# Top-k attention and two feed-forward layers on one core: float64 weights converted through PSUM, attention outputs in the score banks

## The chip, the cores and the metric

The kernel runs on one core of one Trainium2 chip. The metric is the device time of one execution in microseconds (us). Five instruction queues run side by side, each in its own fixed order: TensorE (PE, with its weight loads shown apart as PEld), VectorE (DVE), ScalarE (ACT), GpSimd (POOL) and SyncE (SP), which issues the DMAs. An instruction waits for others through semaphores, and everything behind it in its queue waits with it.

## The reference

```python
def _attn_ref(q, k, v):                      # batch 4, heads 8, seq 576, head_dim 64
    scores = scale * np.matmul(q, k.transpose(0, 1, 3, 2))
    kth = np.partition(scores, -32, axis=-1)[..., -32:-31]
    scores = np.where(scores >= kth, scores, -1e9)
    attn = softmax(scores)
    return np.matmul(attn, v).astype(np.float32)
def _moe_ref(x, w_in, w_out):                # 2304 tokens, 512 -> 2048 -> 512
    h = x @ w_in
    return (np.maximum(0.01 * h, h) @ w_out).astype(np.float32)
def _moe2_ref(x, w1, w2, w3, w_out):         # 512 -> 768 -> 512
    h = np.maximum(np.maximum(x @ w1, x @ w2), x @ w3)
    return (h @ w_out).astype(np.float32)
```

The attention output, laid out as 2304 tokens by 512, goes through the two layers one after the other. The weights of both layers come as float64.

## The kernel before, in words

**Attention** is cut into 72 steps. A step takes two score tiles of 128 query rows by 576 keys (two heads of one block of 128 tokens, or four heads of a block of 64). PE computes the scores into the PSUM tile `s`, two banks of which columns 0 to 287 are used (L702); ACT copies them to `S` in SBUF (L707); DVE finds the 32nd largest value of every row by 8 MAX8 and 6 MATCH_REPLACE8 instructions of 576 columns (L722, L724, 14 in all), masks one exponential (L777) and makes a mask for the other (L781); POOL multiplies and splits (L784, L788); a transposing DMA makes `pt` (L791); PE multiplies by V into the PSUM tile `av`, one bank (L816 to L818); DVE makes the reciprocals `r` of the row sums from it (L823, L825), and ACT scales it into `xs` (L827).

**The feed-forward layers** run in 10 units of 128 to 256 tokens. Each has a phase H (PE: `h<-xu,wi`, then `acc<-f16t,wo`) and a phase M (PE: `h<-k,w`, a maximum over three products on DVE at L1000, then `acc<-f16t,w`). PE multiplies in two-part float16 (`three`, L859 to L861). Unit 0 begins phase H only when all chunks of `w_in` and `w_out` are ready, and phase M only when those of w1, w2, w3 and the second `w_out` are; phase H of unit 1 waits for the last of these too.

**The weights** come in 42 pieces: 16 of 1024 columns (kinds "i" and "o", `w_in` and `w_out`), 18 of 512 (kind "t") and 8 of 384 (kind "z"). `prep_w` loads a piece as 64-bit words (L478) and makes float32 bits of it by three integer instructions on DVE, each over the whole piece, which read every second 32-bit word of it: L484 (one tensor in, a shift and an and), L487 and L490 (two tensors in: the loaded words and the result so far). All operands lie in SBUF. ACT and PE then find a norm (L505, L511), DVE reduces it (L516, L326), POOL makes a scale of it (`pow2`, L333), and ACT and POOL write the two float16 parts (`split3`, L352 to L354).

**The order** of every queue is set by the planner `Plan`. Each `op` has an engine, an estimated duration, keys that it reads and writes and a priority; `run` simulates the queues and writes the instructions in the order of their simulated starts. Buffers are limited by `NB`. For a weight instruction the estimate is `dve(n)`, with its first argument the columns. The planner treats `s` and `av` as two buffers; which instruction waits for which in the built program is found afterwards, from the memory that they touch, by the framework under it.

PSUM has 8 banks of 512 float32 columns: `s` 2, `av` 1, `acc` 2, `h` 3. The tiles `h` serve the products, and the small sums of `total` and the norms as well.

Of the kernel before, what the change touches and what calls it, by code (L numbers as in the profile page):

```python
# [9 lines left out]
F32 = mybir.dt.float32  # L10
# [17 lines left out]
PS = 2048.0  # L28
# [191 lines left out]
def attention_moe_kernel(ctx, tc, qk, v, w_in, w_out, w123, w2o, outT):  # L220
# [11 lines left out]
          "s": 1, "av": 1, "acc": 2, "h": 3, "junk": 1, "xcap": 2, "pr": 8, "ph": 4, "ra": 3, "fi": 6, "ft": 9, "rw": 3, "fz": 3, "rc": 2, "hH": 3, "hM": 3, "kH": 2, "kM": 5, "fH": 2, "fM": 2}  # L232
# [45 lines left out]
    NCOL = 318  # L278
    colt = cp.tile([P, NCOL], F32, name="colt")
# [179 lines left out]
    SC = {}  # L459
    PRW0 = -13.5  # L460
    GATES = {1: [("d", 0, 0, 0, 1)], 2: [("d", 0, 1, 0, 1)]}

    def prep_w(kind, c, parts, hi, lo, colnorm, n2c, s, bi, pr, tags, guard=((), (), []), gate=()):
# [8 lines left out]
        for i, saps in enumerate(parts):  # L472
# [3 lines left out]
            for sap, n in saps:  # L476
# [5 lines left out]
                w = lambda raw=raw, n=n: raw().bitcast(I32)[:, :2 * n].rearrange("p (n t) -> p n t", t=2)  # L482
                t = lambda f=f, n=n, o=o: f()[:, o:o + n]
# [3 lines left out]
                op(DVE, dve(n), lambda w=w, t=t: V.scalar_tensor_tensor(  # L487
                    t(), w()[:, :, 0], 29, t(), op0=ALU.logical_shift_right, op1=ALU.bitwise_or),
                   r=[raw] + zr + zf, w=[(f, o)], pr=pr)
                op(DVE, dve(n), lambda w=w, t=t: V.scalar_tensor_tensor(  # L490
                    t(), w()[:, :, 1], -0x40000000, t(), op0=ALU.bitwise_and, op1=ALU.bitwise_or),
                   r=[raw] + zr + zf, w=[(f, o)], pr=pr)
# [187 lines left out]
    def attention(i):  # L680
# [119 lines left out]
        av = lambda: avb()[:, :260].rearrange("p (h e) -> p h e", e=65)  # L800
        for j in range(2):
            vt = VT[b, hps[j]]

            def avm(j=j, vt=vt):
                hs = [(j, slice(0, P), j)] if full else [(hh, slice(64 * hh, 64 * hh + 64), 2 * j + hh)
                                                        for hh in range(2)]
                for hh, qs, a in hs:
                    o = av()[:qs.stop - qs.start, a, :]
# [14 lines left out]
        op(DVE, 0.07, lambda: V.tensor_scalar(r()[:n, 0:nh], av()[:n, 0:nh, 64:65].rearrange("p h e -> p (h e)"),  # L823
                                             1e-9 * PS, None, op0=ALU.add), r=[avb], w=[(r, 0)], pr=pr)
        op(DVE, 0.08, lambda: V.reciprocal(r()[:n, 4:4 + nh], r()[:n, 0:nh]), r=[(r, 0)], w=[(r, 1)], pr=pr)  # L825
        for h in range(nh):
            op(ACT, act(64, True, 1), lambda h=h: A.activation(xs()[:n, h], av()[:n, h, 0:64], AF.Copy,  # L827
                                                              scale=r()[:n, 4 + h:5 + h]),
               r=[avb, (r, 1)], w=[(xs, h)], pr=pr)
# [343 lines left out]
```

## Time and profile before

| | |
|---|---|
| median of 3 runs | 1165.75 us (1165.68 to 1166.59) |
| the profiled execution | 1165.0 us, span of its trace 1163.2 us |
| busy in that span | PE 923.0, DVE 998.8, ACT 758.5, POOL 728.9 us |
| mean granted TensorE clock | 0.899 of full speed |

Busy times are sums over the span, so the table says nothing of when an engine was busy; the stretches in the rows below do. A line number is that of the kernel before; `w`, `k`, `raw` are names of SBUF tiles, `colt` a tile of single columns.

### The profile page before, as it was taken

How to read it: one execution, taken by the hardware profiler on the slowest of the kernel's cores; microseconds unless marked ns; L12 is line 12 of the kernel's file. 1: busy time of each engine (PE TensorE's matmuls, PEld its weight loads, DVE VectorE, ACT ScalarE, POOL GpSimd, SP SyncE). 2: the span in 40 equal slices, each digit the busy share in tenths (PEclk: the TensorE clock that was granted, in tenths of full speed). 3: DMA queues.
4: the chain of work that ended last, by engine and by line, in shares of the span. 5: the costliest groups of instructions: out<-in, count | busy, mean ns of one | idle time of the engine just before them, and what ended most of it. 6: DMA issues, size and time to landing. Idle time of an engine off the chain costs nothing.

```text
span 1163.2 us, 27290 instructions
## 1 busy us (share of the span) xinstructions
PE 923.0 (79%) x10294; PEld 807.4 (69%) x10294; DVE 998.8 (86%) x2106; ACT 758.5 (65%) x1625; POOL 728.9 (63%) x1054
## 2 busy tenths in 40 slices
PE   3252234675389899789899978998999999999998
PEld 2131223664289788678788867887988898898987
DVE  3999999999999999899996999989989999994001
ACT  7666566777567766547777865677787667564341
POOL 5577885797546766547777664567787557464231
PEclk9965555796589999899999999999999999999999
DMA  7756518554563543334466433554473332332000
GB/s 229 250 150 219 181 25 234 158 140 113 123 148 66 103 81 69 63 71 117 95 163 160 86 73 61 101 128 107 98 177 87 82 82 55 69 69 56 15 1 19
DMA packets 268548, 125.78 MB, mean 108 GB/s; under 512 B 237440, under 2 KB 255360, under 8 KB 266368
## 3 DMA queue, kind: packets, MB, share of 16 engines
q1 hardware_dynamic: 268416, 124.04, 43.4%
q8 instruction: 81, 1.33, 0.5%
q14 instruction: 51, 0.42, 0.1%
HBM read 62.65 MB, written 14.16 MB: 66 GB/s over the span
## 4 chain that ended last, share of the span: by engine, by line
PE 51%; DVE 20%; POOL 8%; ACT 7%; DMA 7%; issue 4%; SPq 1%; POOLq 0%; ACTq 0%; DVEq 0%
PE h L859 9%; PE h L860 9%; PE h L861 9%; DMA pt<-phl 6%; PE acc L860 5%; PE acc L861 5%; PE acc L859 5%; DVE m L722 5%; DVE w L724 4%; PE s L702 3%; DVE w L487 3%; DVE w L490 2%; POOL phl L788 2%; PE av L816 2%; DVE w L484 2%
## 5 line engine op out<-in xcount | busy, mean ns | idle before, releaser
L722 DVE MAX8 m<-w 128x8 f32<-128x576 f32 x432 | 310.2, 747 | 0.3
L916 POOL TENSOR_TENSOR f16t<-k,f16t 128x256 f16<-128x256 f32 (+2 forms) x220 | 143.4, 654 | 183.6 <-ACT f16t L910 174.9
L788 POOL TENSOR_TENSOR phl<-pp,phl 128x576 f16<-128x576 f32 x144 | 189.8, 1325 | 36.3 <-ACT phl L786 35.2
L724 DVE MATCH_REPLACE8 w<-m,w 128x576 f32<-128x576 f32 x288 | 212.1, 741 | 0.0
L859 PE MATMUL h<-k,w 128*128 128x256 f16 (+2 forms) x720 | 189.9, 268 | 22.1 <-ACT k L956 8.3
L860 PE MATMUL h<-k,w 128*128 128x256 f16 (+2 forms) x720 | 190.0, 268 | 5.2 <-POOL k L958 4.8
L861 PE MATMUL h<-k,w 128*128 128x256 f16 (+2 forms) x720 | 190.1, 268 | 0.0
L860 PE MATMUL acc<-f16t,wo 128*128 128x256 f16 (+2 forms) x640 | 167.3, 265 | 7.7 <-POOL f16t L916 7.7
L859 PE MATMUL acc<-f16t,wo 128*128 128x256 f16 (+2 forms) x640 | 167.4, 265 | 0.7 <-ACT f16t L910 0.7
L861 PE MATMUL acc<-f16t,wo 128*128 128x256 f16 (+2 forms) x640 | 167.3, 265 | 0.0
L859 PE MATMUL h<-xu,wi 128*128 128x256 f16 (+1 forms) x576 | 156.2, 271 | 4.4 <-ACT k L903 3.7
L702 PE MATMUL s<-kt,qt 128*128 128x288 f16 (+5 forms) x800 | 109.6, 287 | 60.0 <-ACT S L707 45.2
L860 PE MATMUL h<-xu,wi 128*128 128x256 f16 (+1 forms) x576 | 156.3, 271 | 0.0
L861 PE MATMUL h<-xu,wi 128*128 128x256 f16 (+1 forms) x576 | 156.2, 271 | 0.0
L786 ACT ACTIVATE phl<-pp 128x576 f16<-128x576 f32 x144 | 97.0, 681 | 63.4 <-DVE pp L777 24.0
L772 ACT ACTIVATE pp<-S,nb,colt 128x576 f32<-128x576 f32 x144 | 121.7, 860 | 16.3 <-POOL nb L762 11.3
L784 POOL TENSOR_TENSOR pp<-pp,S 128x576 f32<-128x576 f32 x72 | 93.7, 1301 | 58.3 <-DVE S L781 34.8
L910 ACT ACTIVATE f16t<-k 128x256 f16<-128x256 f32 (+2 forms) x220 | 85.7, 392 | 58.5 <-DVE k L1000 55.8
L860 PEld LDWEIGHTS <-w 128*128 128x128 f16 x960 | 95.3, 99 | 36.8 <-issue 27.9
L702 PEld LDWEIGHTS <-qt 128*128 128x128 f16 (+1 forms) x800 | 64.5, 109 | 79.4 <-issue 54.9
L903 ACT ACTIVATE k<-h,colt 128x256 f32<-128x256 f32 (+2 forms) x160 | 71.3, 449 | 69.9 <-PE h L861 67.8
L707 ACT ACTIVATE S<-s 128x576 f32<-128x576 f32 x144 | 92.7, 644 | 36.0 <-PE s L702 30.0
(136 smaller groups left out, 2709.4 us busy)
## 6 DMA issues: line engine op xcount, KB each, us to landing
w<-in_w SPq DMA_DIRECT2D x18, 512.0 KB, 4.4
w<-in_w_in SPq DMA_DIRECT2D x8, 1024.0 KB, 7.5
w<-in_w_out SPq DMA_DIRECT2D x8, 1024.0 KB, 4.9
raw<-in_qk SPq DMA_DIRECT2D x24, 288.0 KB, 3.3
dqk<-hl SPq DMA_DIRECT2D x48, 144.0 KB, 2.5
kt<-dqk SPq DMA_DIRECT2D x16, 288.0 KB, 3.2
qt<-dqk SPq DMA_DIRECT2D x144, 32.0 KB, 2.3
raw<-in_v SPq DMA_DIRECT2D x12, 352.0 KB, 3.6
```

The costliest lines, as they stand in the source:

```text
L702: T.matmul(p()[osl, h, o:o + w], q()[:, hh, st, :n], k()[:, hh, kc:kc + w], start=st == 0, stop=st == 1, skip_group_check=True)
L707: op(ACT, act(S, True), lambda t=t, p=p: A.activation(t().rearrange("p (a s) -> p a s", a=2), p()[:, :, :288], AF.Copy), r=[p], w=[(Sp, j) ...
L722: op(DVE, dve(S) * 1.03, lambda mc=mc, src=src: V.max(mc(), src()), r=rd, w=[(m, j, 0, r)], pr=pd)
L724: op(DVE, dve(S) * 1.03 + 0.06, lambda mc=mc, src=src, j=j: V.match_replace(out=wj(j), in_to_replace=mc(), in_values=src(), imm_value=NEG) ...
L772: op(ACT, act(S, aps=2), lambda j=j, es=es: A.activation(pp()[:, j], Sb[j](), AF.Exp, bias=nb()[:, j:j + 1], scale=es[:, 0:1]), r=[(Sp, j) ...
L784: op(POOL, pool(S), lambda j=j: G.tensor_tensor(p2(j), p2(j), mk(j), op=ALU.mult), r=[(Sp, j)], w=[(pp, j)], pr=pr)
L786: op(ACT, act(S), lambda j=j: A.activation(phl()[:, 0, j], pp()[:, j], AF.Copy), r=[(pp, j)], w=[(phl, 0, j)], pr=pr)
L788: op(POOL, pool(S), lambda j=j: G.tensor_tensor(phl()[:, 1, j], pp()[:, j], phl()[:, 0, j], op=ALU.subtract), r=[(pp, j), (phl, 0, j)], w= ...
L859: T.matmul(out, wt(0), xt(0), start=first, stop=False, skip_group_check=True)
L860: T.matmul(out, wt(0), xt(1), start=False, stop=False, skip_group_check=True)
L861: T.matmul(out, wt(1), xt(0), start=False, stop=last, skip_group_check=True)
L916: op(POOL, pool(N) + 0.044, lambda: G.tensor_tensor(hl()[:, 1, :N], g()[:, 0, :N], hl()[:, 0, :N], op=ALU.subtract), r=[(g, 0), (hl, 0)], ...
```

## The change

Three things change. The first two of the three integer instructions of every weight piece now write into PSUM instead of SBUF, and the second and third read their second tensor from there; the third still writes the float32 result to SBUF. Pieces of 1024 columns are converted in two halves, with 6 instructions instead of 3. Kinds "i" and "o" use the two `acc` banks for it, "t" and "z" one bank of `h` at a time (the new limit `hW`). To make room, the tile `av` is gone: `s` and `av` become views of one tile `sav` of two banks, scores in columns 0 to 287, outputs of the attention in columns 288 to 417 of each bank. The freed bank makes the fourth of `h`. The planner's estimate for a converting instruction is raised by 0.06 us, and the first of the three loses its estimate as a fast one.

```diff
-          "s": 1, "av": 1, "acc": 2, "h": 3, ... "hH": 3, "hM": 3, "kH": 2, ...
+          "s": 1, "av": 1, "acc": 2, "h": 4, ... "hH": 3, "hM": 3, "hW": 1, "kH": 2, ...
...
+    sav = ps.tile([P, 2, 512], F32, name="sav")
+    ZONE["s"] = [sav[:, :, :288]]
+    ZONE["av"] = [sav[:, :, 288:418]]
...
+    CVK = "iotz"
+    CW = 512
+    CVX = 0.06
...
-                op(DVE, dve(n, True), lambda w=w, t=t: V.tensor_scalar(
-                    t(), w()[:, :, 1], 3, 0x3FFFFFFF, op0=ALU.logical_shift_left, op1=ALU.bitwise_and),
-                   r=[raw] + zr + zf, w=[(f, o)], pr=pr)
...
+                for q in range(0, n, CW):
+                    cw = min(CW, n - q)
...
+                    if kind in CVK:
+                        pb = buf("acc", [P, 2, UN]) if kind in "io" else fbuf("h", "W", [P, 512])
...
+                    op(DVE, dve(cw, pb is None) + CVX * (pb is not None), lambda w=w, m=m: V.tensor_scalar(
+                        m(), w()[:, :, 1], 3, 0x3FFFFFFF, op0=ALU.logical_shift_left, op1=ALU.bitwise_and),
+                       r=[raw] + zr + zf, w=mk_, pr=pr)
+                    op(DVE, dve(cw) + CVX * (pb is not None), lambda w=w, m=m: V.scalar_tensor_tensor(
+                        m(), w()[:, :, 0], 29, m(), op0=ALU.logical_shift_right, op1=ALU.bitwise_or),
+                       r=[raw] + zr + zf, w=mk_, pr=pr)
+                    op(DVE, dve(cw) + CVX * (pb is not None), lambda w=w, t=t, m=m: V.scalar_tensor_tensor(
+                        t(), w()[:, :, 1], -0x40000000, m(), op0=ALU.bitwise_and, op1=ALU.bitwise_or),
+                       r=[raw] + zr + zf + mk_ * (pb is not None), w=[(f, o)], pr=pr)
...
-        av = lambda: avb()[:, :260].rearrange("p (h e) -> p h e", e=65)
+        av = lambda: avb().rearrange("p x (h e) -> p x h e", e=65)
+        avh = lambda a: av()[:, a // 2, a % 2] if not full else av()[:, 0, a]
```

Lines move by 3 to 15: L484, L487, L490 become L498, L501, L504; L722 and L724 become L736 and L738; L777 becomes L791; L823 becomes L838; L707 becomes L721; L827 becomes L842.

The order of the queues changes in many places, since the planner's estimates do. On DVE, while `w_in` and `w_out` are converted, the kernel before has top-k instructions (`m_799`, `w_862`) among the conversions of the `w_out` pieces (`w_77<-w_76`):

```order
L484 TENSOR_SCALAR w_77<-w_76 128x1024
L516 TENSOR_REDUCE colt<-h_936 128x1
L487 SCALAR_TENSOR_TENSOR w_77<-w_76,w_77 128x1024
L326 TENSOR_SCALAR colt<-colt 128x1
L587 TENSOR_REDUCE colt<-colt 128x1
L490 SCALAR_TENSOR_TENSOR w_77<-w_76,w_77 128x1024
L329 TENSOR_SCALAR colt<-colt 128x1
L606 TENSOR_REDUCE colt<-colt 128x1
L724 MATCH_REPLACE w_862<-m_799,w_862 128x576
```

In the changed kernel the same stage reads as follows (`acc` are the PSUM banks):

```order
L498 TENSOR_SCALAR acc_1058<-w_76 128x512
L498 TENSOR_SCALAR acc_1066<-w_76 128x512
L501 SCALAR_TENSOR_TENSOR acc_1058<-w_76,acc_1058 128x512
L501 SCALAR_TENSOR_TENSOR acc_1066<-w_76,acc_1066 128x512
L504 SCALAR_TENSOR_TENSOR w_77<-w_76,acc_1058 128x512
L530 TENSOR_REDUCE colt<-h_1061 128x1
L504 SCALAR_TENSOR_TENSOR w_77<-w_76,acc_1066 128x512
L329 TENSOR_SCALAR colt<-colt 128x1
L498 TENSOR_SCALAR acc_1096<-w_76 128x512
```

The last 13 of the 16 pieces of "i" and "o" now stand nearly back to back, with 4 top-k instructions among them, and the last of them comes after 61 of the 1008 top-k instructions where it came after 74.

On DVE at the end of the weights, the kernel before has this around the last piece of "z" (`w_77<-raw_2755` stands for a "z" piece; the very last one writes `raw` in the same way, after 193 top-k instructions and before the 14th L777):

```order
L490 SCALAR_TENSOR_TENSOR w_77<-raw_2693,w_77 128x384
L722 MAX m_2612<-w_2627 128x8
L724 MATCH_REPLACE w_2627<-m_2612,w_2627 128x576
L781 TENSOR_SCALAR S_1741<-S_1741,m_2421 128x2x288
L484 TENSOR_SCALAR w_77<-raw_2755 128x384
L724 MATCH_REPLACE w_2627<-m_2612,w_2627 128x576
L487 SCALAR_TENSOR_TENSOR w_77<-raw_2755,w_77 128x384
```

In the changed kernel the very last piece stands behind the 14th L791 (the former L777), after 197 top-k instructions:

```order
L838 TENSOR_SCALAR r_3125<-sav 128x2
L791 SCALAR_TENSOR_TENSOR pp_3069<-S_2797,m_3036,pp_3069 128x576
L498 TENSOR_SCALAR h_3128<-raw_3084 128x384
L840 RECIPROCAL r_3125<-r_3125 128x2
L795 TENSOR_SCALAR S_2797<-S_2797,m_3036 128x2x288
L501 SCALAR_TENSOR_TENSOR h_3128<-raw_3084,h_3128 128x384
L736 MAX m_3139<-S_2919 128x8
L504 SCALAR_TENSOR_TENSOR raw_3041<-raw_3084,h_3128 128x384
```

On ACT, late in the program, the kernel before has the copy of the scores (`S<-s`) and the scaling of the attention output (`xs<-av`) like this, with the engines that each waits for in brackets:

```order
L827 ACTIVATE xs_13344<-av_13343,r_13386 128x64 [waits DVE_49,Pool_49]
L827 ACTIVATE xs_13344<-av_13343,r_13386 128x64
L786 ACTIVATE phl_13380<-pp_13268 128x576 [waits Activation_49,Pool_49]
L707 ACTIVATE S_13421<-s_13247 128x576
L833 ACTIVATE xhl_13345<-xs_13344 128x128 [waits DMAHW6_49,Activation_49]
L707 ACTIVATE S_13421<-s_13435 128x576 [waits PE_49]
```

In the changed kernel a copy that stands between an attention output and its scaling waits for DVE, which makes `r` of that output:

```order
L800 ACTIVATE phl_13213<-pp_13145 128x576 [waits DMAHW0_49,DVE_49]
L721 ACTIVATE S_13247<-sav 128x576 [waits PE_49,Pool_49]
L800 ACTIVATE phl_13213<-pp_13145 128x576
L721 ACTIVATE S_13247<-sav 128x576 [waits DVE_49]
L842 ACTIVATE xs_13215<-sav,r_13261 128x64 [waits DVE_49]
L842 ACTIVATE xs_13215<-sav,r_13261 128x64
```

Over the whole program the built order has 20 copies of the scores that wait for an `r`, 20 instructions `r` that wait for a copy of the scores, and 6 that wait for a score product; the kernel before has none of these three kinds of wait. On PE, 42 score products or their weight loads wait for an `r` or an `xs`, where in the kernel before none does and 35 attention products do (5 of them are left).

## Rows read from the trace of the kernel before

**Rows 1.** Busy time by stretch: us, engines (instructions), granted clock, DMA share, GB/s.

```profile
0.00:75.00 75.00, 26.18 (x172) 17.06 (x173) 54.41 (x115) 52.60 (x95) 44.91 (x96) 0.93 0.73 222
75.00:158.00 83.00, 25.70 (x254) 17.94 (x254) 82.15 (x105) 48.97 (x72) 66.74 (x51) 0.50 0.53 167
158.00:320.00 162.00, 84.05 (x846) 72.23 (x844) 157.38 (x319) 111.83 (x227) 117.16 (x153) 0.68 0.53 139
327.00:1053.00 726.00, 679.54 (x7904) 602.04 (x7903) 683.74 (x1520) 503.21 (x1132) 465.24 (x697) 0.98 0.44 97
1053.00:1163.00 110.00, 104.22 (x1088) 95.22 (x1085) 14.14 (x35) 37.24 (x92) 30.14 (x53) 0.98 0.06 16
```

**Rows 2.** The chain that ended last, by engine and by line (page).

```profile
PE 51%; DVE 20%; POOL 8%; ACT 7%; DMA 7%; issue 4%; SPq 1%; POOLq 0%; ACTq 0%; DVEq 0%
PE h L859 9%; PE h L860 9%; PE h L861 9%; DMA pt<-phl 6%; PE acc L860 5%; PE acc L861 5%; PE acc L859 5%; DVE m L722 5%; DVE w L724 4%; PE s L702 3%; DVE w L487 3%; DVE w L490 2%; POOL phl L788 2%; PE av L816 2%; DVE w L484 2%
```

**Rows 3.** First starts of phases H and M: ns min/median/max, first and last start.

```profile
L859 PE MATMUL h<-k,w x720: 216/272/422, 326.9 to 1155.4; 128*128 128x256 f16 x126, 128*128 128x192 f16 x36, 128*128 128x128 f16 x18
...
L859 PE MATMUL h<-xu,wi x576: 242/273/368, 195.5 to 1120.6; 128*128 128x256 f16 x149, 128*128 128x192 f16 x43
```

**Rows 4.** DVE busy in 0 to 330 us: L484, then L487, then L490.

```profile
0.00:330.00 330.00, 35.80 (x42) 0.69 0.57 164
...
0.00:330.00 330.00, 46.18 (x42) 0.69 0.57 164
...
0.00:330.00 330.00, 53.80 (x42) 0.69 0.57 164
```

**Rows 5.** Instructions of L484, L487 and L490: ns min/median/max, first and last start.

```profile
L484 DVE TENSOR_SCALAR w<-w x25: 411/686/2608, 9.3 to 231.6; 128x1024 int32<-128x1024 int32 x16, 128x512 int32<-128x512 int32 x9
...
L487 DVE SCALAR_TENSOR_TENSOR w<-w,w x16: 668/1209/2372, 79.4 to 233.3; 128x512 int32<-128x512 int32 x9, 128x1024 int32<-128x1024 int32 x7
...
L487 DVE SCALAR_TENSOR_TENSOR raw<-raw,raw x2: 535/538/541, 309.2 to 317.8; 128x384 int32<-128x384 int32 x2
...
L490 DVE SCALAR_TENSOR_TENSOR raw<-raw,raw x2: 543/545/547, 310.4 to 319.0; 128x384 int32<-128x384 int32 x2
```

**Rows 6.** DVE and POOL in order of time, 76 to 86 us: start, us.

```profile
76.58 5.97 POOL L354 TENSOR_TENSOR wi<-w,wi 128x1024 f16<-128x1024 f32 x1 [3.03 <-ACT wi L353]
77.61 0.69 DVE L484 TENSOR_SCALAR w<-w 128x1024 int32<-128x1024 int32 x1
78.22 1.22 DVE L490 SCALAR_TENSOR_TENSOR w<-w 128x1024 int32<-128x1024 int32 x1
79.35 1.22 DVE L487 SCALAR_TENSOR_TENSOR w<-w,w 128x1024 int32<-128x1024 int32 x1
...
80.56 2.54 DVE L484 TENSOR_SCALAR w<-w 128x1024 int32<-128x1024 int32 x1
...
83.10 2.21 DVE L490 SCALAR_TENSOR_TENSOR w<-w,w 128x1024 int32<-128x1024 int32 x1
```

**Rows 7.** Other DVE instructions by line: ns min/median/max, first and last start.

```profile
L722 DVE MAX8 m<-w x432: 719/748/762, 28.5 to 1052.9; 128x8 f32<-128x576 f32 x144
...
L777 DVE SCALAR_TENSOR_TENSOR pp<-S,m,pp x72: 790/802/1703, 35.4 to 1053.5; 128x576 f32<-128x576 f32 x72
...
L1000 DVE SCALAR_TENSOR_TENSOR k<-h,colt,k x120: 326/473/485, 331.4 to 1156.0; 128x256 f32<-128x256 f32 x84, 128x192 f32<-128x192 f32 x24, 128x128 f32<-128x128 f32 x12
...
L516 DVE TENSOR_REDUCE colt<-h x22: 199/410/547, 22.9 to 263.5; 128x1 f32<-128x256 f32 x8, 128x1 f32<-128x64 f32 x8, 128x1 f32<-128x384 f32 x6
```

**Rows 8.** What the 16 DMA engines moved, in 40 slices (page).

```profile
GB/s 229 250 150 219 181 25 234 158 140 113 123 148 66 103 81 69 63 71 117 95 163 160 86 73 61 101 128 107 98 177 87 82 82 55 69 69 56 15 1 19
```

**Rows 9.** Who waited for whom: us in total, times, longest.

```profile
PE h L511 <- ACT junk L505: 56.9, 32, 4.7
...
DVE r L823 <- PE av L818: 20.8, 28, 2.6
```

**Rows 10.** The copy of the scores by line: ns min/median/max.

```profile
L707 ACT ACTIVATE S<-s x144: 626/650/676, 26.2 to 1024.8; 128x576 f32<-128x576 f32 x144
```

More of the change, by code (lines that the diff above doesn't have):

```diff
@@ L231, in attention_moe_kernel @@
           "phl": 1, "pt": 1, "r": 2, "xs": 1, "xhl": 1, "f16t": 4, "yj": 1,
[L232 removed]
+          "s": 1, "av": 1, "acc": 2, "h": 4, "junk": 1, "xcap": 2, "pr": 8, "ph": 4, "ra": 3, "fi": 6, "ft": 9, "rw": 3, "fz": 3, "rc": 2, "hH": 3, "hM": 3, "hW": 1, "kH": 2, "kM": 5, "fH": 2, "fM": 2}
     PSUM_TAGS = ("s", "av", "acc", "h")
@@ L490, in prep_w @@
-                op(DVE, dve(n), lambda w=w, t=t: V.scalar_tensor_tensor(
-                    t(), w()[:, :, 1], -0x40000000, t(), op0=ALU.bitwise_and, op1=ALU.bitwise_or),
-                   r=[raw] + zr + zf, w=[(f, o)], pr=pr)
+                for q in range(0, n, CW):
+                    cw = min(CW, n - q)
+                    w = lambda raw=raw, q=q, cw=cw: raw().bitcast(I32)[:, 2 * q:2 * (q + cw)].rearrange("p (n t) -> p n t", t=2)
+                    t = lambda f=f, cw=cw, q=q + o: f()[:, q:q + cw]
+                    pb = None
+                    if kind in CVK:
+                        pb = buf("acc", [P, 2, UN]) if kind in "io" else fbuf("h", "W", [P, 512])
+                    m = t if pb is None else (lambda pb=pb, cw=cw, two=kind in "io": (
+                        pb().rearrange("p a n -> p (a n)") if two else pb()).bitcast(I32)[:, :cw])
+                    mk_ = [(f, o)] if pb is None else [pb]
+                    op(DVE, dve(cw, pb is None) + CVX * (pb is not None), lambda w=w, m=m: V.tensor_scalar(
[7 more added lines that the diff above has]
+                       r=[raw] + zr + zf + mk_ * (pb is not None), w=[(f, o)], pr=pr)
@@ L807, in avm @@
                 for hh, qs, a in hs:
-                    o = av()[:qs.stop - qs.start, a, :]
+                    o = avh(a)[:qs.stop - qs.start, :]
                     for c in range(5):
@@ L822, in attention @@
         r = buf("r", [P, 8])
-        op(DVE, 0.07, lambda: V.tensor_scalar(r()[:n, 0:nh], av()[:n, 0:nh, 64:65].rearrange("p h e -> p (h e)"),
-                                             1e-9 * PS, None, op0=ALU.add), r=[avb], w=[(r, 0)], pr=pr)
+        op(DVE, 0.07, lambda: V.tensor_scalar(r()[:n, 0:nh].rearrange("p (x h) -> p x h", h=2),
+                                             av()[:n, 0:nh // 2, :, 64], 1e-9 * PS, None, op0=ALU.add), r=[avb], w=[(r, 0)], pr=pr)
         op(DVE, 0.08, lambda: V.reciprocal(r()[:n, 4:4 + nh], r()[:n, 0:nh]), r=[(r, 0)], w=[(r, 1)], pr=pr)
         for h in range(nh):
-            op(ACT, act(64, True, 1), lambda h=h: A.activation(xs()[:n, h], av()[:n, h, 0:64], AF.Copy,
+            op(ACT, act(64, True, 1), lambda h=h: A.activation(xs()[:n, h], avh(h)[:n, 0:64], AF.Copy,
                                                               scale=r()[:n, 4 + h:5 + h]),
```

5 lines of the change are left out of this document (removed).

## The prediction

> **What bounds the kernel now.** I read the busy time by stretch first. [...] From 327 to 1053 us PE and DVE are both about 94% busy at full clock, and in the last 110 us PE works alone [rows 1]. [...]
>
> The hinge is the start of phase M of unit 0. The last weight piece leaves DVE at 319.5 us [rows 5], the first product of phase M starts at 326.9 [rows 3], and from there PE is idle for only 46.5 + 5.8 = 52 us until the end [rows 1]. Phase H of unit 0 starts at 195.5 [rows 3], over 120 us before its phase M may, so it is not the hinge. So a microsecond that DVE saves before its last weight piece moves the start of the dense part of PE, and the attention steps with it, since they stand behind the weights in the same queue. The rest then keeps its length, unless its waits change.
>
> **What conversion costs now.** The three lines are busy for 35.8, 46.2 and 53.8 us, 135.8 in 126 instructions [rows 4]. Neighbours overlap a little: an instruction of 1.22 us at 78.22 is followed by one at 79.35, 1.13 later [rows 6]. At 0.08 us each, 126 instructions hold the queue for 125.8 us.
>
> Far less would do. The same instruction takes 668 ns for 512 columns at its shortest and up to 2372 for 1024; for 384 it takes 535 to 547 late in the weights [rows 5]. The long ones lie where POOL works: a POOL split of 1024 columns runs 5.97 us while DVE's two-tensor instructions pass, then DVE's take 2.2 and 2.5 us where they had taken 0.7 and 1.2 [rows 6]. Which DVE instructions suffer shows in the spread: L777, two SBUF tensors, goes from 802 to 1703 ns; L722, one SBUF tensor, never passes 762; L1000, one tensor in PSUM and one in SBUF, never passes 485, though POOL is busy two thirds of that time [rows 7, 1]. After the change every converting instruction has one SBUF tensor at most. I take it that all of this waiting goes.
>
> [...]
>
> **What it costs after.** 150 instructions of 512 columns and 24 of 384. Reading PSUM costs next to nothing: L1000 at 256 columns takes 473; L777 minus 320 columns at 1.04 ns is 469 [rows 7]. So a two-tensor instruction is priced as its undisturbed SBUF form, 668 - 80 = 588 and 541 - 80 = 461 ns. The first of the three is different: it runs nearly twice as fast per column now (411 for 512 columns) [rows 5], and no row has it writing PSUM. Ends: it keeps that rate, or it runs like the others. The row nearest to it is L516, one tensor with PSUM at one end, at 1.04 ns a column (64 to 384 columns, 199 to 547) [rows 7]; I take the slow end. The fast one would give back 50 x 0.26 + 8 x 0.2 = 14 us more. Sum: 150 x 0.588 + 24 x 0.461 = 99.3 us. **Conversion: 99.3 - 125.8 = -26.5 us.** Writing to PSUM has no row either: nothing, or at worst the 0.08 of overlap lost at each of the 116 writing instructions, 9 us; I take nothing, as reading costs nothing.
>
> [...]
>
> **What the order costs.** The last weight piece comes after 197 top-k instructions instead of 193, and behind one more L777 and L781. Four at 0.67 (748 less 0.08) and about 1.3 for the two are **+4 us** for the hinge [rows 7]. On the other side 13 pieces of "i" and "o" now stand nearly back to back. DVE needs 13 x 6 x 0.588 = 46 us for them and some 8 for the norms and the four top-k between. They bring 13 x 1.05 MB (128 rows of 1024 words of 8 bytes) = 13.6 MB, and the fastest slices moved 219 to 250 GB/s [rows 8], so 54 to 62 us: the loads become about as long as the work. The norm of a piece, too, comes back through ACT and PE while DVE is already converting the next, and PE waited 57 us for those squares before [rows 9]; DVE stands behind it in L530. Ends: nothing, and 10 us; **+5 us** taken.
>
> **What sharing the banks costs.** Two kinds of wait are new in DVE's and ACT's queues: 20 copies of scores for an `r`, and 26 `r` for a copy or a score product. A copy takes 0.65 us [rows 10], so the ends are 0 and 46 x 0.65 = 30 us. DVE reaches `r` before the product is done in 28 of 72 steps, 20.8 us in all [rows 9]: it follows closely, so a copy that waits for it waits for little more than the product. In the usual row of the changed order the copy stands behind the scaling anyway, as before, and ACT's queue alone holds it. I take 0. Behind a late copy stand the scores of the next step on PE and, in its fixed order, all feed-forward products. The fourth bank of `h` I cost at nothing: phases H and M keep their three; what it gives is room for the conversions and for the sums.
>
> **The sum.** -26.5 + 4 + 5 = -17.5 us. The profiled execution took 1165.0 us, so 1147.5; the median of the runs is 0.75 above it: **1148 us**, 1.5% less.
>
> **The rivals.**
> *The loads and norms take over.* The dense stretch of "i" and "o" is bound by its 13.6 MB or by squares on ACT, each piece costs a wait for the norm, and about half of the saving goes. [...] With 10 us of waits for loads and some 4 more for norms: 1157 us.
> *The shared banks hold PE (slower).* It decides when the 46 waits cost 17.5 / 46 = 0.38 us each on the path, for instance when the copy stands waiting at its place and PE has nothing between. At the whole 0.65: 1148 + 30 = 1178; at 0.5, which I price, 1171 us. For it: PE is 94% busy from 327 us on, so what stops it is not made up [rows 1]. Against it: DVE's short way from the product to `r` [rows 9], and the many products between.
> [...]
> *The change does not lift the waiting.* If the slow instructions wait for something else than the second SBUF tensor, the excess stays: 126 instructions would take 16 x 2.87 + 18 x 1.51 + 8 x 1.2 = 83 us undisturbed, so some 43 of the 125.8 are excess. 99.3 + 43 = 142, 16.5 more than now, with the 4 of the order 1186 us. The flat L1000 and L722 speak against it [rows 7].
>
> **How the numbers follow.** Forecast 0.64 (1140 to 1155: 4 us of unknown writes or a load that is hidden, either way), loads and norms 0.18, shared banks 0.12, no relief 0.04, 0.02 for an order that cancels out. A measurement of this kernel can tell about 0.2%, 2.3 us, from no change. Faster: the first two less a little, 0.81. Slower: 0.09 of the third, 0.04 and a bit of the second, 0.14. Same: 0.05. The range: below, all loads hidden and part of PE's 52 idle us gone because attention is ahead, 8 us: 1148 - 5 - 8 = 1135. Above, writes at their worst (9 us) with the loads' 10: 1148 + 9 + 5 = 1162, and some of the shared banks: 1166. 1135 to 1166.
>
> **What would show it.** Right: L498, L501 and L504 in PSUM forms near 0.67 us for 512 columns with hardly a spread, about 115 us busy together (99.3 with the overlap taken off); POOL splits of the weights near 2.1 us; the first product of phase M near 309 us, and the last L791 near 1035. DVE idle between 75 and 140 us would be the first rival; L716 (the score products) waiting for ACT's copy, ACT's copy for `r`, or PE idle above 60 us from the hinge to the end would be the second; spread durations in the PSUM forms the third. Wrong would also be a hinge that comes early with an end that does not: then the late part is ruled by an order that I have only read, not timed.

## The result and the profile after

The changed kernel takes 1151.97 us (median of 4 runs, 1150.69 to 1154.63) where the kernel before, on the same chip, takes 1165.72 us (1165.59 to 1166.59). The ratio is 0.9902, with a 95% interval of 0.9879 to 0.9925: faster by 1.0%. (The two medians alone would make it 0.988; this text goes by the ratio, so the gain is 11 to 14 us.) The profiled execution took 1152.1 us with a span of 1150.2, where the one before took 1165.0 with a span of 1163.2: 13 us less. 1148 us was forecast, 17.5 less.

The busy time of the changed kernel by stretch answers to [rows 1]; the columns are the same.

```profile
0.00:75.00 75.00, 26.40 (x172) 17.54 (x173) 53.93 (x120) 53.15 (x96) 42.31 (x96) 1.00 0.75 225
75.00:158.00 83.00, 25.87 (x238) 16.94 (x237) 78.92 (x170) 57.46 (x81) 48.78 (x63) 1.00 0.57 171
158.00:320.00 162.00, 88.12 (x950) 75.77 (x951) 150.57 (x331) 112.16 (x237) 101.29 (x151) 0.73 0.54 149
327.00:1053.00 726.00, 673.75 (x7948) 598.15 (x7946) 675.25 (x1500) 497.79 (x1124) 462.28 (x701) 1.00 0.44 94
1053.00:1150.00 97.00, 91.23 (x914) 82.51 (x911) 9.53 (x25) 31.17 (x76) 22.69 (x40) 1.00 0.07 18
```

DVE has more idle time in both early stretches from 75 us on: 4.1 and 11.4 us, where it had 0.9 and 4.6. In the dense part, from 327 us, it is busy for 8 us less than before. PE does not stand idle less there either: 52.3 + 5.8 us against 46.5 + 5.8.

The converting instructions, L498, L501 and L504, answer to [rows 5]: ns min/median/max, first and last start, forms.

```profile
L498 DVE TENSOR_SCALAR acc<-w x32: 677/684/695, 9.8 to 134.8; 128x512 int32<-128x512 int32 x32
...
L501 DVE SCALAR_TENSOR_TENSOR acc<-w,acc x32: 673/685/696, 11.0 to 135.9; 128x512 int32<-128x512 int32 x32
...
L504 DVE SCALAR_TENSOR_TENSOR w<-w,acc x32: 664/677/681, 12.2 to 137.3; 128x512 int32<-128x512 int32 x32
...
L504 DVE SCALAR_TENSOR_TENSOR raw<-raw,h x2: 530/532/534, 299.2 to 306.6; 128x384 int32<-128x384 int32 x2
```

The spread is gone: minimum and maximum of one shape lie within 5% of each other. In the kernel before, one shape of L487 had 1210 and 3028 ns (the row x16 of [rows 5] holds two shapes, so its 668 and 2372 are not of one):

```profile
L487 DVE SCALAR_TENSOR_TENSOR w<-w x9: 1210/1226/3028, 10.0 to 146.9; 128x1024 int32<-128x1024 int32 x9
```

Who the partner was can be counted over the trace of before: 60 of the 126 converting instructions take over a tenth longer than the shortest of their operation and shape, and every one of the 60 runs beside a POOL instruction; of the other 66, 43 do. The first of the three, which took 411 ns for 512 columns at its best [rows 5], now takes 684. Their busy time in the first 330 us, L498, L501 and L504 in turn, answers to [rows 4]:

```profile
0.00:330.00 330.00, 37.23 (x58) 0.87 0.59 171
...
0.00:330.00 330.00, 37.38 (x58) 0.87 0.59 171
...
0.00:330.00 330.00, 38.00 (x58) 0.87 0.59 171
```

That is 112.6 us in 174 instructions. In these three rows the overlap of two instructions of one line, the two halves of a piece, is already taken off; the single durations add up to 115.2 us, and less the overlap of 0.08 each (one of 0.67 us at 62.01 us is followed by the next at 62.60) they hold the queue for 101 us, where 126 were held before. The other side of the contention is free as well: the POOL splits of `w_in`, of which one took 5.97 us [rows 6], now all take the same time.

```profile
L357 POOL TENSOR_TENSOR wi<-w,wi x8: 2128/2135/2141, 29.7 to 114.3; 128x1024 f16<-128x1024 f32 x8
```

The first starts of the phases answer to [rows 3], and the last masking of an exponential, L791, to the L777 of [rows 7]:

```profile
L874 PE MATMUL h<-k,w x720: 216/272/421, 316.8 to 1142.4; 128*128 128x256 f16 x126, 128*128 128x192 f16 x36, 128*128 128x128 f16 x18
...
L874 PE MATMUL h<-xu,wi x576: 242/272/368, 181.8 to 1107.6; 128*128 128x256 f16 x149, 128*128 128x192 f16 x43
...
L791 DVE SCALAR_TENSOR_TENSOR pp<-S,m,pp x72: 779/804/1698, 34.7 to 1046.7; 128x576 f32<-128x576 f32 x72
```

Phase H begins 13.7 us earlier, phase M 10.1 earlier (316.8 for 326.9), and the attention ends 6.8 earlier (1046.7 for 1053.5). The conversion gave 25 us to DVE's queue, and two fifths of that arrived at the hinge, the start of phase M.

Where the rest went, the waits say. DVE's waits for the attention products, over the whole span, answer to [rows 9]: us in total, times, longest.

```profile
DVE r L838 <- PE sav L833: 40.7, 37, 2.8
...
DVE r L838 <- PE sav L716: 9.6, 6, 2.3
...
DVE r L838 <- ACT S L721: 2.1, 2, 1.1
```

These are 52.4 us, where the kernel before had 20.8 in one row. Two of the three rows, 11.7 us, are new: `r` waiting for score products and for copies of scores, which no kernel with separate banks shows. The growth of the first row, from 20.8 to 40.7, is no such sign: two kernels below with a new order and no shared bank have 38.5 and 34.5 us there. PE's waits from 327 to 1045 us show the partner:

```profile
PE sav L831 <- DMA pt<-phl: 18.5, 22, 1.6
PE sav L716 <- ACT S L721: 11.2, 16, 1.6
```

The same two rows of the kernel before, L816 for the transposed weights and L702 for the copy, held 8.1 and 6.3 us. And in the chain that ended last, the transposing DMA `pt<-phl` has doubled its share, from 6% [rows 2] to 12%:

```profile
PE 40%; DMA 14%; DVE 11%; POOL 7%; ACT 6%; issue 5%; SPq 1%; POOLq 0%; ACTq 0%; DVEq 0%
DMA pt<-phl 12%; PE h L874 7%; PE h L875 7%; PE h L876 7%; PE acc L875 4%; DVE m L736 4%; PE acc L874 4%; PE acc L876 4%; DVE w L738 3%; PE sav L716 3%; POOL phl L802 3%; PE sav L831 2%; PE sav L832 2%; PE sav L833 2%; POOL f16t L931 1%
```

The transposes are hardly slower (a median of 4.3 us from issue to landing, 4.0 before); they are waited for more often. So the attention steps run one behind another more than they did. How much of this the shared banks did and how much the new order, these rows do not say: the same two kernels wait 14.8 and 19.3 us for the transposes in the same stretch.

### The profile page after: what moved, and what is told of

Read it like the earlier page. It is cut to its first block, busy times and chain, and to the rows that moved or that the text cites. A ratio compares the mean times of both kernels' runs of the same rounds, so it can differ in the third digit from the quotient of the medians.

```text
span 1150.2 us, 27408 instructions
## 1 busy us (share of the span) xinstructions
PE 912.4 (79%) x10294; PEld 797.7 (69%) x10294; DVE 973.6 (85%) x2154; ACT 757.3 (66%) x1625; POOL 680.6 (59%) x1054
## 4 chain that ended last, share of the span: by engine, by line
PE 40%; DMA 14%; DVE 11%; POOL 7%; ACT 6%; issue 5%; SPq 1%; POOLq 0%; ACTq 0%; DVEq 0%
DMA pt<-phl 12%; PE h L874 7%; PE h L875 7%; PE h L876 7%; PE acc L875 4%; DVE m L736 4%; PE acc L874 4%; PE acc L876 4%; DVE w L738 3%; PE sav L716 3%; POOL phl L802 3%; PE sav L831 2%; PE sav L832 2%; PE sav L833 2%; POOL f16t L931 1%
## 5 line engine op out<-in xcount | busy, mean ns | idle before, releaser
L736 DVE MAX8 m<-w 128x8 f32<-128x576 f32 x432 | 309.7, 746 | 0.1
L738 DVE MATCH_REPLACE8 w<-m,w 128x576 f32<-128x576 f32 x288 | 211.9, 741 | 0.0
L802 POOL TENSOR_TENSOR phl<-pp,phl 128x576 f16<-128x576 f32 x144 | 183.7, 1281 | 45.5 <-ACT phl L800 43.9
L874 PE MATMUL h<-k,w 128*128 128x256 f16 (+2 forms) x720 | 187.0, 264 | 7.8 <-ACT k L971 5.5
L875 PE MATMUL h<-k,w 128*128 128x256 f16 (+2 forms) x720 | 186.9, 264 | 3.7 <-POOL k L973 3.6
L876 PE MATMUL h<-k,w 128*128 128x256 f16 (+2 forms) x720 | 186.8, 264 | 0.0
L716 PE MATMUL sav<-kt,qt 128*128 128x288 f16 (+5 forms) x800 | 110.1, 288 | 77.1 <-ACT S L721 56.2
L875 PE MATMUL acc<-f16t,wo 128*128 128x256 f16 (+2 forms) x640 | 164.9, 262 | 4.7 <-POOL f16t L931 4.6
L874 PE MATMUL acc<-f16t,wo 128*128 128x256 f16 (+2 forms) x640 | 165.0, 262 | 0.0
L876 PE MATMUL acc<-f16t,wo 128*128 128x256 f16 (+2 forms) x640 | 165.0, 262 | 0.0
L716 PEld LDWEIGHTS <-qt 128*128 128x128 f16 (+1 forms) x800 | 65.2, 109 | 99.8 <-issue 75.9
L831 PE MATMUL sav<-vt,pt 128*128 128x65 f16 (+1 forms) x800 | 91.2, 202 | 38.5 <-DMA pt<-phl 34.1
L721 ACT ACTIVATE S<-sav 128x576 f32<-128x576 f32 x144 | 92.8, 644 | 32.2 <-PE sav L716 18.4
```

What stands on the lines that cost most here:

```text
L716: T.matmul(p()[osl, h, o:o + w], q()[:, hh, st, :n], k()[:, hh, kc:kc + w], start=st == 0, stop=st == 1, skip_group_check=True)
L721: op(ACT, act(S, True), lambda t=t, p=p: A.activation(t().rearrange("p (a s) -> p a s", a=2), p()[:, :, :288], AF.Copy), r=[p], w=[(Sp, j) ...
L736: op(DVE, dve(S) * 1.03, lambda mc=mc, src=src: V.max(mc(), src()), r=rd, w=[(m, j, 0, r)], pr=pd)
L738: op(DVE, dve(S) * 1.03 + 0.06, lambda mc=mc, src=src, j=j: V.match_replace(out=wj(j), in_to_replace=mc(), in_values=src(), imm_value=NEG) ...
L802: op(POOL, pool(S), lambda j=j: G.tensor_tensor(phl()[:, 1, j], pp()[:, j], phl()[:, 0, j], op=ALU.subtract), r=[(pp, j), (phl, 0, j)], w= ...
L831: T.matmul(o, hc, vh, start=c == 0, stop=False, skip_group_check=True)
```

## The experiments

Theory A: the conversion through PSUM brings the gain, by taking the contention between DVE and POOL away, and the shared banks give a part of it back. Rival B: the gain comes from the planner's new estimates and the order that they make. Rival C: the fourth bank of `h` is what helps. Each ratio is to the kernel before, timed on the same chip; 0.01 of it is 11.65 us. Differences between two kernels are taken between ratios, and by the intervals each is known to 3 to 6 us.

**Sharing alone.** The kernel before, with `s` and `av` as views of one tile of two banks; its queues keep their order.

```diff
+    sav = ps.tile([P, 2, 512], F32, name="sav")
+    ZONE["s"] = [sav[:, :, :288]]
+    ZONE["av"] = [sav[:, :, 288:418]]
...
-        av = lambda: avb()[:, :260].rearrange("p (h e) -> p h e", e=65)
+        av = lambda: avb().rearrange("p x (h e) -> p x h e", e=65)
+        avh = lambda a: av()[:, a // 2, a % 2] if not full else av()[:, 0, a]
```

> The kernel before with nothing changed but the two views: scores and attention outputs in one tile of two banks. The planner knows nothing of it, so every queue keeps the order of the kernel before. Theory A (the shared banks cost waits: DVE for its r instructions, PE for its score products): slower than before by 4 to 12 us, 1170 to 1178 us, with more idle time of DVE before L823's successor than the 20.8 us of before. Rival (my price of nothing in the prediction): within 2 us of 1165.7.

Measured: 1182.14 us, ratio 1.0158 (1.0122 to 1.0193), 18 us more than before. DVE's waits of this kernel over the span:

```profile
DVE r L827 <- PE sav L822: 15.8, 19, 2.6
...
DVE r L827 <- PE sav L705: 12.0, 9, 2.1
DVE m L725 <- ACT S L710: 9.4, 7, 3.4
DVE r L827 <- ACT S L710: 5.5, 7, 1.8
```

The two rows of conflict, on score products (L705) and their copies (L710), hold 17.5 us, of which a part takes the place of waiting for the attention product (15.8 instead of 20.8). The first product of phase M starts at 333.2, 6.3 late, and the last masking at 1073.8, 20 late: 6 of the 20 us of this execution are lost ahead of phase M and 14 behind it. My price of 0 for the shared banks is off by the whole 18 us, and the 4 to 12 us of theory A were too few as well.

**The changed kernel with its conversion in SBUF.** The order, the pieces of 512 columns, the four banks and the shared banks stay; only the place of the intermediate results changes, to the columns that the third instruction will write.

```diff
+                    def m(f=f, cw=cw, q=q + o):
+                        if f.ap is None:
+                            f.ap = f.make()
+                        return f()[:, q:q + cw]
```

> The changed kernel in its own order, instruction by instruction, in pieces of 512 columns, but the two intermediate results of each conversion stay in SBUF. Theory A (the gain is the waiting for POOL that PSUM operands avoid): the three converting lines are busy 140 to 160 us instead of 112.6, with durations spread up to over 2 us, and the whole takes 1170 to 1185 us. Rival B (the gain comes from the new order and the fourth h bank): within 4 us of 1152.

Measured: 1180.22 us, ratio 1.0152 (1.0118 to 1.0187). PSUM against SBUF in the same order is 0.0250, 29 us. The spread is back (one form of each line, ns min/median/max):

```profile
L504 DVE TENSOR_SCALAR w<-w x41: 406/420/2286, 9.3 to 237.1; 128x512 int32<-128x512 int32 x41
...
L507 DVE SCALAR_TENSOR_TENSOR w<-w,w x23: 671/681/2611, 87.0 to 238.3; 128x512 int32<-128x512 int32 x23
...
L510 DVE SCALAR_TENSOR_TENSOR w<-w,w x23: 668/680/1746, 88.2 to 239.9; 128x512 int32<-128x512 int32 x23
```

The converting lines are busy for 42.1 + 44.9 + 44.2 = 131.2 us instead of 112.6, although the first of them has its fast form again. That is 19 of the 29 us. POOL loses as well, busy for 713.8 us over the span instead of 680.6. As before, every converting instruction that takes over a tenth longer than the shortest of its kind (49 of 174) runs beside a POOL instruction. What reaches the path shows at the hinge:

```profile
L880 PE MATMUL h<-k,w x720: 218/272/421, 342.3 to 1167.3; 128*128 128x256 f16 x126, 128*128 128x192 f16 x36, 128*128 128x128 f16 x18
```

Phase M begins 25.5 us later than in the changed kernel (316.8), and from there to the end both take the same, 832.8 us here and 833.4 there: all that the place of the intermediate results is worth lies ahead of phase M. The new place brings no new wait at the first instruction either: L504 waits for loads alone, 4.2 us, where L498 had 4.3.

A second thing follows from the pair: this kernel and the one before it differ in order, pieces and the fourth bank, and take the same time, 1180 and 1182 us, known to 6 us. As the changed kernel uses them, these three are worth nothing measurable together.

**The conversion through PSUM, with `av` in a bank of its own.** The room comes from `h`, which has three banks again.

```diff
-          "s": 1, "av": 1, "acc": 2, "h": 4, ...
+          "s": 1, "av": 1, "acc": 2, "h": 3, ...
...
-    sav = ps.tile([P, 2, 512], F32, name="sav")
-    ZONE["s"] = [sav[:, :, :288]]
-    ZONE["av"] = [sav[:, :, 288:418]]
...
-        av = lambda: avb().rearrange("p x (h e) -> p x h e", e=65)
+        av = lambda: avb()[:, :260].rearrange("p (x h e) -> p x h e", h=2, e=65)
```

> The changed kernel with the attention outputs back in a bank of their own and three h banks instead of four; conversions through PSUM as changed. The planner's order moves. Theory A: the waits of the shared banks go, 1140 to 1149 us, and DVE idles under 25 us before r. Rival C (sharing is free, and the fourth bank of h is worth something): 1152 or above.

Measured: 1155.92 us, ratio 0.9932 (0.9904 to 0.9960): faster than before, but not faster than the changed kernel. The expectation missed twice: the time, and the idle time of DVE before `r`, which was to fall under 25 us:

```profile
DVE r L835 <- PE av L830: 38.5, 42, 3.2
```

So long waits of `r` for the attention product come with a new order, shared banks or not (the fifth experiment, whose banks are not shared either, has 34.5 us of them). Its conversion is as quick as in the changed kernel, yet ends no earlier than before:

```profile
L501 DVE SCALAR_TENSOR_TENSOR raw<-raw,h x2: 533/533/533, 310.7 to 319.4; 128x384 int32<-128x384 int32 x2
```

Phase M starts at 329.5. Here the planner puts attention steps ahead of the last weights: the 14th masking comes at 296.5 us (321.7 before), and the weights wait their turn. With three banks of `h` the conversions of "t" and "z" compete for one with phase H; that this is why the planner sets them later was not tried alone.

**The changed kernel, with the planner told of the shared banks.** A buffer `sb` with one slot, which the scores and the attention outputs both take: the planner then never lets a score product begin while an attention output is not yet scaled, and the reverse.

```diff
+          "sb": 1, ...
-    plan = Plan(NB, {"raw", "av", "junk", "hl", "k2", "h", "f16t", "rc"})
+    plan = Plan(NB, {"raw", "av", "junk", "hl", "k2", "h", "f16t", "rc", "sb"})
...
             p = buf("s", [P, 2, 512])
+            p.also = (plan.buf("sb", lambda: 1),)
...
         avb = buf("av", [P, 512])
+        avb.also = (plan.buf("sb", lambda: 1),)
```

> The changed kernel, whose planner is told that scores and attention outputs can't hold the shared banks at the same time (one more buffer, sb, that both take). The planner's order moves. Theory A: DVE no longer waits for a score product before r, PE stands less at the copies, 1143 to 1150 us. Rival C: no change beyond 2 us of 1152, since the waits were hidden; a variant of A in which the exclusion makes the pipeline of attention shorter would show as 1155 to 1165.

Measured: 1124.80 us, ratio 0.9666 (0.9637 to 0.9695), 27 us less than the changed kernel and well below the range expected. Its conversion, its first product of phase M and its last masking:

```profile
L504 DVE SCALAR_TENSOR_TENSOR raw<-raw,h x2: 532/532/533, 279.9 to 287.0; 128x384 int32<-128x384 int32 x2
...
L876 PE MATMUL h<-k,w x720: 216/272/421, 294.9 to 1112.7; 128*128 128x256 f16 x126, 128*128 128x192 f16 x36, 128*128 128x128 f16 x18
...
L792 DVE SCALAR_TENSOR_TENSOR pp<-S,m,pp x72: 790/803/1858, 34.2 to 1015.2; 128x576 f32<-128x576 f32 x72
```

Phase M starts 22 us earlier than in the changed kernel, the attention ends 31 us earlier. No score product and no copy is among what DVE's `r` waits for; of the rows of before one is left, and less of it than before the change:

```profile
DVE r L840 <- PE sav L835: 17.5, 34, 2.1
```

In the trace no copy waits for an `r` any more (7 did, for 7.2 us); attention products wait for copies instead, 7.8 us from 327 to 1045 us (2.7 in the changed kernel). The waits of PE for the transposed weights, from 327 to 1045 us, fall from 18.5 to 2.8 us, and the chain is one of products again:

```profile
PE 56%; DVE 18%; ACT 8%; POOL 6%; DMA 6%; issue 4%; SPq 1%; POOLq 0%; ACTq 0%; DVEq 0%
PE h L876 9%; PE h L877 9%; PE h L878 9%; DVE m L737 6%; PE acc L876 6%; PE acc L877 6%; PE acc L878 6%; DVE w L739 5%; PE sav L717 4%; DMA pt<-phl 2%; PE sav L833 2%; PE sav L834 2%; PE sav L835 2%; DVE pp L792 1%; POOL pp L799 1%
```

**The planner's estimates alone.** The kernel before, with only the estimates of the three instructions raised as in the change.

```diff
+    def est(n):
+        return max(1, n // 512) * (dve(min(n, 512)) + 0.06)
...
-                op(DVE, dve(n, True), lambda w=w, t=t: V.tensor_scalar(
+                op(DVE, est(n), lambda w=w, t=t: V.tensor_scalar(
...
-                op(DVE, dve(n), lambda w=w, t=t: V.scalar_tensor_tensor(
+                op(DVE, est(n), lambda w=w, t=t: V.scalar_tensor_tensor(
```

> The kernel before, conversions in SBUF and all banks as they were; only the planner's estimates of the converting instructions are raised to those of the changed kernel, so the order of the queues moves. Theory A (order by itself is worth nothing, the saving is the waiting for POOL): 1158 to 1172 us, conversions still busy over 125 us. Rival B (estimates nearer to the measured times give the gain): below 1155 us.

Measured: 1184.63 us, ratio 1.0181 (1.0136 to 1.0226). Rival B falls as far as estimates go: by themselves they make the order worse, beyond theory A's range too. The run shows something else too: an order planned anew can move this kernel by 20 us with no instruction changed. So a single kernel with a new order proves little, above and below; what counts is whether two pairs say the same.

**Sharing in the kernel before, with the planner told.** The edits of the first experiment and the buffer `sb`; the conversion stays in SBUF, `h` has three banks.

> The kernel before with scores and attention outputs in the shared banks and the planner told of it; conversions stay in SBUF, three banks of h. If the 18 us that the shared banks cost are waits that the planner did not know of, they come back: 1158 to 1168 us. If telling the planner is worth more than that by itself, as the step from 1152 to 1125 suggests, below 1150 us. If the exclusion costs the pipeline something that the fourth bank of h had paid for: above 1172 us.

Measured: 1161.08 us, ratio 0.9971 (0.9955 to 0.9987), 22 us less than with sharing untold. Telling the planner is worth 22 us here and 27 us in the changed kernel: two pairs, one answer. Two banks for three are not dear; an order made as if they were three is.

**Three banks of `h` in the told kernel.**

```diff
-          "s": 1, "av": 1, "acc": 2, "h": 4, ...
+          "s": 1, "av": 1, "acc": 2, "h": 3, ...
```

> The fastest version so far (changed kernel, planner told of the shared banks) with three banks of h instead of four; one bank of PSUM lies idle. Theory D (the fourth bank matters, because conversions of the second layer's weights take one bank of h while phase H of unit 0 holds three): 1135 to 1150 us, with the last weight piece leaving DVE 10 us or more later than the 287 us of that version. Rival (my price of nothing for the fourth bank): within 4 us of 1125.

Measured: 1148.12 us, ratio 0.9850 (0.9830 to 0.9871): without the fourth bank 21 us of the told kernel's time are lost. PE's waits in this kernel, from 294 us to its end:

```profile
PE h L876 <- ACT k L1013: 9.4, 5, 3.3
PE h L876 <- DVE k L1017: 8.3, 12, 1.1
```

L1013 and L1017 read the `h` banks of phase M, so PE waits there for a bank to come free. With four banks, in the same stretch, L1013 is waited for 2.2 us, and L1017 does not stand among the nine largest waits, of which that is the smallest. (The largest wait with three banks is another: attention products wait 18.3 us for copies of scores, 7.8 with four.)

Theory D of the expectation is met as well, in its time and in its sign. The last weight piece leaves DVE 17 us later than with four banks (287.0):

```profile
L504 DVE SCALAR_TENSOR_TENSOR raw<-raw,h x2: 534/536/537, 296.6 to 303.9; 128x384 int32<-128x384 int32 x2
```

PE waits 9.4 us for converting instructions that read a bank of `h` (L504), 2.0 with four. Phase M begins at 310.2 us for 294.9, and takes 839.1 us from there to the end for 825.7: about half of the loss lies ahead of phase M, in the room for the conversions, and half behind it. The dense part shows the second half (from 320 to 1000 us, columns as in [rows 1]); first the kernel with three banks,

```profile
320.00:1000.00 680.00, 632.36 (x7286) 558.10 (x7284) 638.30 (x1419) 469.28 (x1044) 431.76 (x650) 0.98 0.45 97
```

then the one with four:

```profile
320.00:1000.00 680.00, 641.61 (x7494) 571.17 (x7492) 654.73 (x1446) 480.50 (x1076) 448.51 (x671) 0.98 0.45 97
```

DVE and PE do 16 and 9 us more work in the same 680 us. The changed kernel, which has the fourth bank too, had 633.4 us of DVE there; that the waits of the untold banks kept it from using the bank fits, and was not shown apart.

**The told kernel with the old estimate.** `CVX` is 0 instead of 0.06, so a PSUM form costs in the plan what an SBUF form with two tensors costs.

> The fastest version so far with the planner's surcharge of 0.06 us per converting instruction taken out, since the trace shows 677 ns busy, 0.60 us from start to start, which is the bare estimate. If estimates that fit are worth something: 1112 to 1121 us. If the order is not that fine: within 5 us of 1125, either side.

Measured: 1121.93 us, ratio 0.9632 (0.9613 to 0.9651), the fastest of all. Against 0.9666 the intervals overlap; whether the estimate is worth anything stays open, and it is not the source of the gain.

**Is the fourth bank room for the conversions?** The told kernel of before (conversion in SBUF), with four banks of `h`.

```diff
-          "s": 1, "av": 1, "acc": 2, "h": 3, ...
+          "s": 1, "av": 1, "acc": 2, "h": 4, ...
```

> Conversion in SBUF as in the kernel before, shared banks with the planner told, and the fourth bank of h (three took 1161.1 us). If the fourth bank's 23 us are room for the conversions, which here need no PSUM: 1155 to 1165 us. If the bank helps the work of the feed-forward phases and the sums by itself: 1135 to 1147 us.

Measured: 1145.06 us, ratio 0.9839 (0.9811 to 0.9868), against 0.9971 with three: 15 us with no conversion in PSUM at all. Here the bank gives nothing ahead of phase M, which begins at 327.2 us (321.2 with three), and 22 us behind it (815.5 us to the end for 837.9). So the bank helps the feed-forward phases and the sums by itself; a kernel that converts through PSUM uses it as room for that too. Rival C is half right: the bank helps in a plan that knows of the shared banks, and in the changed kernel's plan no gain of it shows.

**The told kernel with its conversion in SBUF.** The same edit as in the second experiment, on the told kernel: its order, other places for the intermediate results.

> The order of the kernel with four banks of h and the planner told (1124.8 us), with the intermediate results of the conversion in SBUF. If taking the contention away is worth the same 28 us here as in the changed kernel: 1148 to 1158 us. If a good order hides part of it: 1130 to 1145 us.

Measured: 1159.94 us, ratio 0.9959 (0.9933 to 0.9985), against 0.9666: 34 us. That is a little above the first forecast, and the second falls: taking the contention away is worth no less in the better order. Again it lies ahead of phase M, which begins at 329.7 us for 294.9, with 828.3 and 825.7 us from there to the end.

The effects side by side, each pair known to 3 to 6 us:

| | pairs | us |
|---|---|---|
| conversion in PSUM, order kept | untold; told | -29; -34 |
| conversion in PSUM, order planned anew, told | three banks; four banks | -14; -20 |
| conversion in PSUM, order planned anew, banks not shared | kernel before; `av` in its own bank | -8 |
| planner told of the shared banks | SBUF, three banks; PSUM, four | -22; -27 |
| fourth bank of `h`, told | SBUF; PSUM | -15; -21 |

## Why the prediction was right, and where it was not

The forecast, "1148 us", with the conversion as its reason, came within 4 us of the time, inside the likeliest case. Its cause, the conversion, is the right one. That the sum came so near is in part luck: of its five terms only the largest is shown right, and errors of both signs in the others nearly cancelled.

**The conversion, -26.5 us.** Right in size and cause. Predicted were forms "near 0.67 us for 512 columns with hardly a spread, about 115 us busy together (99.3 with the overlap taken off)", and POOL splits near 2.1 us; measured 0.68, 115.2 (101) and 2.13. The slow end that I took for the first of the three instructions was the true one, and writing to PSUM costs hardly anything (medians of 684 and 685 ns into PSUM, 677 into SBUF). The whole of it in time, with the order kept, is 29 us: a little more than the queue's 25, within what the pair can tell. Both sides of the contention show in this pair: POOL's splits of `w_in` take 2128 to 2141 ns beside PSUM forms and 2122 to 2712 beside SBUF forms, the two-tensor instructions of DVE, for 512 columns, at most 697 ns with PSUM and up to 2611 without. That one SBUF tensor at most would end the waiting for the first of the three as well was my estimate: it reads one tensor with its result in SBUF too, and there took up to 2286 ns for 512 columns in the second experiment; with its result in PSUM it takes 672 to 695. The rival that the waiting has another cause falls with the spread. One reading of a row was off without harm: L516's own ends, 199 and 547 ns, give 1.09 ns a column, and the 1.04 that I used is what 668 and 535 ns of L487 give [rows 5].

**The order, +4 us, and the loads and norms, +5 us.** DVE waited at L498 for loads of `in_w` 1.9 us and of `in_w_in` 1.8 over the whole span (1.5 and 1.3 at L484 before), and from 75 to 158 us for norms (L530) 0.9 us; over the whole span the waits for norms went from 3.7 to 5.8. Together that is 3 us more than before, of which about 1 falls in the stretch that the term of 5 us was for, and the rival built on it never came near. The longest wait of DVE in that stretch was another, 2.2 us of an `r` for a score product. The four us of the order were not measured apart from the rest.

**Sharing the banks, 0.** This is the step that failed. I wrote that "a copy that waits for it waits for little more than the product", looked for the price on ACT's copies, and took the lower of my two ends, 0 and 30 us. Sharing alone costs 18 us in the order of the kernel before (in the changed kernel's order it was not priced alone, as no bank is left to undo it), and the slower rival, which I gave 0.12 and in which the 46 waits are worth 0.5 us each, 23 us, had nearly its true price. Of the signs that I named for it two were seen: `L716` waiting for ACT's copy (11.2 us, 6.3 before) and ACT's copy waiting for `r` (7.2 us). The third came near: PE idle for 58 us from the hinge on (60 was the bound named, 52 the value before). Where I looked was not wholly right: DVE waits longer than the copies do, 11.7 us for score products and copies. An instruction that waits 2 us in DVE's queue holds the top-k of another step, and with it the masking, the transpose and the product after it; that the steps behind run later for this reason is argued from the order of the queues, and what the runs show is the 18 us.

**The fourth bank, 0.** Nothing in the changed kernel contradicts it, where order, pieces and bank together are worth nothing measurable, but it is wrong as a statement about the bank. "Phases H and M keep their three" is what the limits say, but norms, sums and the other unit's phase draw on the same banks, and PE waited 17.7 us at phase M behind the readers of its banks with three, where one of the two rows is 2.2 us with four and the other too small to be shown. The conversions draw on them as well: PE waited 9.4 us behind L504 with three banks and 2.0 with four. That the order that knew nothing of the shared banks spent this again in the changed kernel is a reading, not shown.

**The sum.** Measured, from pairs: sharing untold +18, conversion -29, and about nothing for order, pieces and bank together; -11, as the ratio says. Mine was -26.5 + 4 + 5 + 0 + 0 = -17.5. The 9 us that I put on order and loads did the work of half the 18 that I left out, and that is the luck in it.

**The hinge.** The reading that DVE's last weight piece moves the dense part held in kind: 12.4 us earlier (306.6 for 319.0), phase M 10.1 earlier, and from there to the end the span is 833.4 us where it was 836.3. I had phase M "near 309" and it began at 316.8; the 7.8 us missing lie within the 10 us by which DVE's idle time from 75 to 320 us grew. Most of that growth is waiting before `r`, 9.2 us in that stretch where it was 1.6. Of it 2.2 are on a score product and so the price of the shared banks; the 7.0 on attention products may be the new order's, as the kernel with `av` in a bank of its own has 9.0 there. The last L791, which I had "near 1035", came at 1046.7: as a hinge for the attention the last weight piece was wrong. The 14th masking came 17.9 us earlier than before, as the forecast would have it, and the 58 steps after it took 742.9 us instead of 731.8. "The rest then keeps its length, unless its waits change" - they changed.

What stays open: why an order planned anew takes back half of what the PSUM conversion gives with the order kept (-14 and -20 against -29 and -34) and, with banks not shared, leaves 8 us of it. That an order made for slow conversions hides them is not what the pair with four banks shows: with the conversion in SBUF and an order made for it, phase M begins 32 us later than with PSUM, as late as with the order kept, and what is given back lies behind it, 815.5 us to the end for 825.7. With three banks phase M begins only 11 us apart, and the rest is about as long (837.9 and 839.1). And no run separates either from the 20 us by which a new order may move the time anyhow. That `av` and `s` could be kept apart in time by another rule than a single slot was not tried.

## What to carry to other kernels

When an edit makes two buffers share a resource, whatever plans the order must hear of it: here the same two banks cost 18 us in an order made without that knowledge, and nothing measurable against the old layout in one made with it. A price of zero for a new wait, argued from the average distance of its two ends, is worth one run of that edit alone, because a forecast may land close by errors that cancel. And the spread between minimum and maximum of one instruction shape was the sign of contention in this profile: 1210 to 3028 ns for 1024 columns of L487 and the like told of 25 us of queue time, which moving one operand out of SBUF gave back as worked out. A row that mixes shapes shows a spread of its own, so it is read by shape.

## What the runs showed of the hardware that was not expected

The first converting instruction loses its fast form, 411 to 684 ns for 512 columns, when its result goes to PSUM, and the whole is still faster by 29 us: the waiting beside POOL, which the SBUF forms have (up to 2286 ns for this instruction in the second experiment, 2611 for the next) and the PSUM forms have not (at most 697), was dearer than the rate.

The granted clock from 75 to 158 us was 0.50 in the trace of before and 1.00 in that of the changed kernel, though PE was busy for as long ahead of it (26.18 and 26.40 us in the first 75 us) and in it (25.70 and 25.87); how the work lay within the stretches was not compared. The time does not follow the clock: the four runs of the changed kernel have mean granted clocks of 0.960, 0.912, 0.958 and 0.951, and took 1152.1, 1151.8, 1150.7 and 1154.6 us. DVE is busy for 79 of these 83 us and PE for 26, so PE is not what bounds that stretch.
